# One pool of six places for the weight blocks and the transposed x, x fetched tile by tile, and the last sums in five PSUM tiles

## The chip, the cores and the metric

The kernel runs on one NeuronCore of a Trainium2 chip, in float32 throughout. The metric is the device time of one execution in microseconds (us). Three runs of the kernel before took 891.31, 893.44 and 893.68 us, so their median is 893.44. TensorE (PE in the profile, with PEld for its weight loads) does the matrix products, VectorE (DVE) most sums and transposes of 32x32 blocks, ScalarE (ACT) copies and squares, GpSimd (POOL) a share of the sums. SyncE (SP) issues the transfers (DMAs): they go out in the order of the program on SP, each waiting for its place in SBUF and for one of eight lanes, so that a DMA does not go before the DMA eight places ahead of it has landed.

## The reference: what is computed

```python
kv  = np.einsum('bhsd,bhse->bhde', k, v)          # 8 batches, 8 heads, 576 tokens, 64
out = np.einsum('bhsd,bhde->bhse', q, kv)
rms = np.sqrt(np.mean(out * out, axis=-1, keepdims=True) + 1e-06)
x   = (out / rms * g_norm)                        # put together to 4608 x 512
h   = x @ w_in                                    # 512 x 2048
g   = np.maximum(h, 0.0) ** 2
y   = g @ w_out                                   # 2048 x 512
```

Linear attention without a softmax, a norm over each head, and a two-layer network with a squared ReLU.

## The kernel before, in words

The 4608 tokens are 36 tiles of 128, and four tiles make a strip, so there are nine strips, zero to eight. Each strip goes "up" (x times w_in, then the squared ReLU) and "down" (times w_out). To save products, matrices are cut into quarters and seven products of sums take the place of eight, at one level or at two. Strip zero goes up plainly and down with one level. Strip one goes up with one level (order of the seven products: 1, 2, 6, 5, 7, 3, 4) and down with two levels, 49 small products (`down_deep`, L1084; the outer seven in `DEEP_ORDER` = 4, 1, 2, 6, 5, 7, 3, each with seven inner ones in two steps: j = 1, 2, 3 and j = 4, 5, 6, 7). Strips two to eight use two levels in both directions; their up runs in 55 slots. The attention of the strips to come, the transposes of q, the key-value products, norms and transfers are put between by lists: `slices` (L690 to L737) holds the attention's steps in order and `attend` runs the next ones; a slot plan with assumed costs decides how many go in one slot.

The first 131 us also convert the weights: sums of quarters of w_in and w_out are made on VectorE and GpSimd and stored to DRAM (w_in_deep, w_out, w_deep), from where blocks are streamed later.

`stream` (L922) asks for the next block of that stream. A block takes a place of 8 KB in each partition from `stream_pool`, which has four. A deep down needs two blocks for each outer product p: one of w_out (768 KB, for j = 3, 1, 2; called (s, p, 0) here) and one of w_deep (1 MB, for j = 5, 6, 7, 4; called (s, p, 1)). An up product of the later strips needs one block of w_in_deep (768 KB). `down_deep` calls `stream()` at each of its steps, behind that step's products (L1110).

The transposed x of a strip (`xT`, L622) has a pool of its own, two places of 8 KB in each partition, so one strip is read while the next is written. For strips zero and one TensorE transposes x (`features`, L627). From strip two on VectorE transposes blocks of 32x32 (`squares_x`), the tile goes to DRAM (`send_x`, L646, 256 KB), and later `fetch_x` (L651) brings it back with four DMAs of 64 KB in the layout that the products need. When a fetch is due is set by a clock that counts steps: 18 units after the store for the tiles of strip two, 6 for later ones. q for coming batches arrives in pairs of DMAs ("drips") when the clock allows and no fetch of x is due.

From strip one on, PSUM holds five tiles for products (`fpsum`) and two, one of double size, for the attention (`apsum`). The seven inner products of one p lie in two PSUM tiles (`PLACE`, and `LAST_PLACE` for the end of strip eight, L1040); `together` (L1061) puts them together on ScalarE and VectorE to `o_sb`, and `send` (L946) stores it. At the end of strip eight the inner products of the last p run in the groups (1), (2, 6, 5, 7), (4, 3), sums between them, and one store of 256 KB ends the kernel.

Of the kernel before, what the change touches and what calls it, by code (L numbers as in the profile page):

```python
# [10 lines left out]
FP32 = mybir.dt.float32  # L11
# [4 lines left out]
ALU = mybir.AluOpType  # L16
# [4 lines left out]
def kernel(  # L21
# [35 lines left out]
    P = 128  # L57
# [28 lines left out]
    xt_pool = ctx.enter_context(tc.tile_pool(name="xt", bufs=2))  # L86
# [4 lines left out]
    conv = ExitStack()  # L91
    raw_pool = conv.enter_context(tc.tile_pool(name="raw", bufs=8))
# [529 lines left out]
    def open_xt(s):  # L622
        if s not in xt:
            xt[s] = xt_pool.tile([P, STRIP // SQ, NP, SQ], FP32, name="xT", tag="xT")
        return xt[s]
# [20 lines left out]
    def send_x(n):  # L646
        d = sent[n] = dram.tile([P, 4, NP, SQ], FP32, name="x_d", tag="x_d", bufs=2 * NT)
        nc.sync.dma_start(out=d, in_=squared.pop(n))
        tiles_due.append((clock[0] + (6 if n >= DEEP_UP * NT + NT else 18), fetch_x, (n,)))
# [53 lines left out]
    slices += [(T, (2, 2)), (features, (last[0],)), (T, (2, 3)), (K, (2, 2, 3))]  # L703
# [239 lines left out]
    def out_tile():  # L943
        return c_pool.tile([P, 2, DH], FP32, name="o_sb", tag="c")

    def send(s, th, eh, o):  # L946
        for i, (part, t, rows) in enumerate(out_rows(NT * s + 2 * th)):
            eng = nc.scalar if i % 2 and s == N_STRIP - 1 and (th, eh) == (0, 1) else nc.sync
            eng.dma_start(out=rows[:, :, ts(eh, DH)], in_=o[part, t, :])
# [90 lines left out]
    LAST_PLACE = {1: (1, 0), 2: (0, 0), 6: (0, 1), 5: (0, 2), 7: (0, 3), 3: (1, 1), 4: (1, 2)}  # L1040
    place = lambda s, p: LAST_PLACE if s == N_STRIP - 1 and p in (5, 3) else PLACE

    def small_products(s, p, js):
        c = "B" if p in (4, 2, 5, 3) else "A"
        if js[0] == 1 and p not in (6, 7, 3):
            opened[c] = set()
            chain[c] = [fpsum.tile([P, 4, P], FP32, name=f"ps_{c}", tag="f") for _ in range(2)]
        for j in js:
            x, i = place(s, p)[j]
            a, w = leaf[p][j], w_blk.pop((s, p, j))  # L1050
            for f in range(FQ // 2):
                nc.tensor.matmul(  # L1052
                    chain[c][x][:, i, :], lhsT=a[:, f, :], rhs=w[:, f, :],
                    start=x not in opened[c] and f == 0, stop=f == FQ // 2 - 1, skip_group_check=True,
                )
            opened[c].add(x)

    def together(s, p):

        def small(j, n=1):  # L1060
            x, i = place(s, p)[j]  # L1061
            return chain["B" if p in (4, 2, 5, 3) else "A"][x][:, i : i + n]
# [12 lines left out]
        yield  # L1075
        add(q[:, 0:4:3], q[:, 0:4:3], small(3, 2))
# [7 lines left out]
    def down_deep(s, k, i):  # L1084
        p = DEEP_ORDER[k]
        if s == N_STRIP - 1 and k == 6 and i == 1:

            steps = together(s, p)
            for js in ((1,), (2, 6, 5, 7), (4, 3)):
                small_products(s, p, js)  # L1090
                next(steps)
            return
# [17 lines left out]
        stream()  # L1110
# [187 lines left out]
    for s in range(N_STRIP):  # L1298
# [25 lines left out]
        for i, (w, fn, a) in enumerate(steps):  # L1324
# [16 lines left out]
            elif s == 0 and i == n_up:  # L1341
                convert(len(conversions))
                conv.close()

                stream_pool = ctx.enter_context(tc.tile_pool(name="stream", bufs=4, reuse_waits="tile"))
                sum_pool = ctx.enter_context(tc.tile_pool(name="sum", bufs=8, reuse_waits="tile"))
# [40 lines left out]
            if i == n_up:  # L1387
                stream(2)
            if i in (n_up + 8, n_up + 11):
                load(2, (i - n_up) // 11, nc.sync, "q")  # L1390
# [9 lines left out]
            if i == n_up + 6:  # L1400
                stream()
# [42 lines left out]
```

## Time and profile before

| what | us |
|---|---|
| median of three runs | 893.44 |
| the profiled execution's own time | 889.28 |
| span of its instructions | 887.3 |
| TensorE products, busy | 876.6 (99%) |
| TensorE weight loads, busy | 821.8 (93%) |
| VectorE, busy | 721.4 (81%) |
| ScalarE, busy | 352.3 (40%) |
| GpSimd, busy | 307.3 (35%) |

The span runs from the first to the last instruction of the profiled execution; 2.0 us lie around it. The DMA engines move 235.73 MB in it, a mean of 266 GB/s, and are busy for most of the time in every stretch. A wait is told as "engine, tile, line <- what released it: us in total, times, the longest". The chain is the work that ended last, followed back from the end; in a timeline each line has the start, the time, the engine and line, the operation and the count.

### The profile page before, as it was taken

Reading aid. Unit: us, or ns where it says so; the run is one execution under the profiler, and the core shown is the slowest. Engines: PE = TensorE matmul, PEld = TensorE weight load, DVE = VectorE, ACT = ScalarE, POOL = GpSimd, SP = SyncE. Lnnn points to the kernel's source line nnn. Section 1 sums busy time; section 2 is a strip of 40 time slices with the busy share of each in tenths; the row PEclk is TensorE's granted clock in tenths of the full one; section 3 lists DMA queues with packets and bytes.
Section 4 is the critical chain, followed back from the end, with each engine's and each line's share of the span. In section 5 each row is a group of like instructions: output and inputs, shape, how many; then the busy total and the mean of one; then the engine's idle time right before and its main releaser. Section 6 shows DMA issues by size and latency. Waiting matters only on the chain.

```text
span 887.3 us, 20876 instructions
## 1 busy us (share of the span) xinstructions
PE 876.6 (99%) x8296; PEld 821.8 (93%) x8296; DVE 721.4 (81%) x1233; ACT 352.3 (40%) x806; POOL 307.3 (35%) x315
## 2 busy tenths in 40 slices
PE   8999999999999999999999999999999999999998
PEld 7445888889999999999999999999999999999998
DVE  4999998879768986798678966897888778876886
ACT  4898242320048303740365034902491147102710
POOL 0000005610558223731474045604470447044700
PEclk9999999999999999999999999999999999999999
DMA  9998997989999888979887988898658864884385
GB/s 314 315 316 251 304 366 234 273 305 328 327 232 262 297 309 249 237 269 331 238 222 250 321 268 247 251 307 285 211 166 309 297 181 171 309 291 155 137 313 180
DMA packets 169953, 235.73 MB, mean 266 GB/s; under 512 B 79488, under 2 KB 134272, under 8 KB 161536
## 3 DMA queue, kind: packets, MB, share of 16 engines
q1 hardware_dynamic: 169696, 234.40, 82.3%
q8 instruction: 65, 1.06, 0.5%
q14 instruction: 32, 0.26, 0.1%
q10 hardware_dynamic: 160, 0.00, 0.0%
HBM read 197.66 MB, written 36.70 MB: 264 GB/s over the span
## 4 chain that ended last, share of the span: by engine, by line
PE 82%; DVE 10%; DMA 3%; ACT 3%; issue 2%; SPq 0%; POOL 0%; DVEq 0%; POOLq 0%; ACTq 0%
PE ps_B L1052 22%; PE ps_A L1248 19%; PE ps_A L1052 16%; PE ps_B L1248 9%; PE ps_C L1248 5%; PE ps_A L835 4%; PE kv_ps L432 2%; PE x_ps L468 2%; DVE w_c L269 2%; PE ps_B L835 1%; DMA w_deep<-w_t 1%; DVE w_t L289 1%; DVE wt L289 1%; PE ps_C L835 1%; DVE w_c L263 1%
## 5 line engine op out<-in xcount | busy, mean ns | idle before, releaser
L1052 PE MATMUL ps_B<-w_blk,g_s 128*128 128x128 f32 x1024 | 126.1, 275 | 0.0
L1052 PEld LDWEIGHTS ps_B<-w_blk,g_s 128*128 128x128 f32 x1024 | 120.0, 192 | 0.1
L1248 PE MATMUL ps_A<-x_l,w_in 128*128 128x128 f32 x784 | 103.8, 275 | 0.3 <-ACT snap L1265 0.3
L1052 PE MATMUL ps_B<-w_blk,gt 128*128 128x128 f32 x768 | 97.5, 275 | 1.5 <-DMA w_blk<-w_out 1.5
L289 POOL TENSOR_TENSOR x_l<-xT 128x256 f32<-128x256 f32 x21 | 15.4, 734 | 238.6 <-PE ps_A L1052 187.9
L1248 PEld LDWEIGHTS ps_A<-x_l,w_in 128*128 128x128 f32 x784 | 95.4, 192 | 0.6 <-ACT snap L1265 0.5
L1052 PE MATMUL ps_A<-w_blk,g_s 128*128 128x128 f32 x768 | 93.6, 275 | 0.0
L1052 PEld LDWEIGHTS ps_B<-w_blk,gt 128*128 128x128 f32 x768 | 91.5, 192 | 1.7 <-DMA w_blk<-w_out 1.7
L1052 PEld LDWEIGHTS ps_A<-w_blk,g_s 128*128 128x128 f32 x768 | 89.6, 192 | 0.0
L1260 POOL TENSOR_TENSOR snap<-snap,gt 128x512 f32<-128x512 f32 x35 | 45.9, 1310 | 119.2 <-ACT snap L1265 103.7
L1265 ACT COPY snap<-ps_A 128x512 f32<-128x512 f32 x63 | 36.9, 585 | 109.5 <-PE ps_A L1248 96.2
L1198 ACT ACTIVATE gt<-gt 128x512 f32<-128x512 f32 x112 | 70.1, 626 | 12.8 <-DVE gt L1260 12.6
L1052 PE MATMUL ps_A<-w_blk,gt 128*128 128x128 f32 x576 | 72.2, 275 | 0.0
L1199 ACT ACTIVATE gt<-gt 128x512 f32<-128x512 f32 x112 | 70.7, 631 | 3.6
L1052 PEld LDWEIGHTS ps_A<-w_blk,gt 128*128 128x128 f32 x576 | 68.2, 192 | 0.0
L1067 DVE TENSOR_TENSOR o_sb<-o_sb,ps_B 128x256 f32<-128x256 f32 (+1 forms) x128 | 49.4, 386 | 19.2 <-ACT o_sb L1068 11.8
L1068 ACT COPY o_sb<-ps_A 128x128 f32<-128x128 f32 x24 | 6.4, 265 | 145.7 <-PE ps_A L1052 145.7
L1154 POOL TENSOR_TENSOR w_i<-w_in 128x512 f32<-128x512 f32 x7 | 10.7, 1524 | 148.1 <-DMA q<-in_q_dram 140.8
L289 DVE TENSOR_TENSOR gt<-gt 128x2048 f32<-128x2048 f32 (+1 forms) x29 | 59.7, 2063 | 0.0
L1260 POOL TENSOR_TENSOR gt<-gt,snap 128x512 f32<-128x512 f32 x42 | 52.4, 1277 | 17.6 <-DVE snap L1260 17.4
L1248 PE MATMUL ps_B<-x_l,w_blk 128*128 128x128 f32 x392 | 52.1, 276 | 0.0
L1248 PE MATMUL ps_A<-x_l,w_blk 128*128 128x128 f32 x392 | 51.9, 275 | 0.0
(183 smaller groups left out, 1835.0 us busy)
## 6 DMA issues: line engine op xcount, KB each, us to landing
w_blk<-w_deep SPq DMA_DIRECT2D x56, 1024.0 KB, 6.5
w_blk<-w_out SPq DMA_DIRECT2D x56, 768.0 KB, 6.0
w_blk<-w_in_deep SPq DMA_DIRECT2D x49, 768.0 KB, 5.5
raw<-in_moe_w_in_dram SPq DMA_DIRECT2D x16, 512.0 KB, 7.0
raw<-in_moe_w_out_dram SPq DMA_DIRECT2D x16, 512.0 KB, 5.8
k<-in_k_dram SPq DMA_DIRECT2D x29, 256.0 KB, 5.2
v<-in_v_dram SPq DMA_DIRECT2D x29, 256.0 KB, 5.4
x_d<-x_q SPq DMA_DIRECT2D x27, 256.0 KB, 5.4
```

The source lines that it names most:

```text
L269: yield nc.vector.scalar_tensor_tensor(out=ci, in0=high, scalar=-(2**30), in1=ci, op0=ALU.bitwise_and, op1=ALU.bitwise_or)
L289: eng.tensor_tensor(out=out, in0=a, in1=b, op=ALU.subtract)
L432: nc.tensor.matmul(ps[ts(h, D), i], lhsT=a, rhs=w, start=i == 0 and c == 0, stop=c == C, skip_group_check=True)
L468: nc.tensor.matmul(ps[half, r, i, ts(p, D)], lhsT=q[row, half], rhs=kvd[b, p][row, row], start=True, stop=True)
L835: nc.tensor.matmul(bank[BANK[p]][:, i, :], lhsT=lhsT(k), rhs=rhs(k), start=p in (1, 5, 2) and i == 0 and k == 0, stop=k == n - 1, skip_gro ...
L1052: nc.tensor.matmul(chain[c][x][:, i, :], lhsT=a[:, f, :], rhs=w[:, f, :], start=x not in opened[c] and f == 0, stop=f == FQ // 2 - 1, skip ...
L1067: add = lambda out, a, b: nc.vector.tensor_tensor(out=out, in0=a, in1=b, op=ALU.add)
L1198: nc.scalar.activation(o, o, AF.Relu)
L1199: nc.scalar.activation(o, o, AF.Square)
L1248: nc.tensor.matmul(ps[:, i, :], lhsT=w, rhs=rhs, start=j in (1, 2, 5) and i == 0, stop=True, skip_group_check=True)
L1260: add = lambda eng, out, a, b: eng.tensor_tensor(out=out, in0=a, in1=b, op=ALU.add)
L1265: nc.scalar.copy(t, ps)
```

## The change

Five parts.

- Places. `xt_pool` becomes a pool of one place that lives only as long as the conversion; strip zero's x lies there. Every later x takes a place of the stream's pool, which has six places in place of four. A one-column memset on GpSimd takes the place for strip one's x as the pool opens.
- Blocks. In strip zero's down one call of `stream()` moves from step 6 to step 4; in `down_deep` one call is added at the first step and those of the last p are left out, so that each block of a deep down is asked for one step earlier. The number of blocks is the same.
- Fetches. The fetch of a tile of strip two is due at its own delay: 6 units for tile 8, 30, 36 and 24 for tiles 9, 10 and 11.
- Order. The transposes of q for the last pair of batch 2, (T, (2, 3)), come before the transposes of x of one tile, features.
- The end. The seven inner products of p = 5 and p = 3 of strip eight lie in five PSUM tiles, three of `fpsum` and two of `apsum`. The last p runs in the groups (1), (2, 6), (5, 7), (4), (3); its sums are added in place as soon as a group ends, and each quarter of 128 x 128 is stored by itself, three from SP and the last from ScalarE's queue.

```diff
--- before.py
+++ after.py
@@ -83,12 +83,12 @@
     rest_pool = ctx.enter_context(tc.tile_pool(name="rest", bufs=1))
     qt_pool = ctx.enter_context(tc.tile_pool(name="qt", bufs=NP + 1))
     xn_pool = ctx.enter_context(tc.tile_pool(name="xn", bufs=3))
-    xt_pool = ctx.enter_context(tc.tile_pool(name="xt", bufs=2))
     small = ctx.enter_context(tc.tile_pool(name="small", bufs=3))
     g_pool = ctx.enter_context(tc.tile_pool(name="g", bufs=4))
     dram = ctx.enter_context(tc.tile_pool(name="dram", bufs=1, space=bass.MemoryType.DRAM))
     c_pool = ctx.enter_context(tc.tile_pool(name="c", bufs=6))
     conv = ExitStack()
+    xt_pool = conv.enter_context(tc.tile_pool(name="xt", bufs=1))
     raw_pool = conv.enter_context(tc.tile_pool(name="raw", bufs=8))
     spare_pool = conv.enter_context(tc.tile_pool(name="spare", bufs=1))
     wtmp = conv.enter_context(tc.tile_pool(name="wtmp", bufs=4))
@@ -621,7 +621,11 @@
 
     def open_xt(s):
         if s not in xt:
-            xt[s] = xt_pool.tile([P, STRIP // SQ, NP, SQ], FP32, name="xT", tag="xT")
+            if s == 0:
+                xt[s] = xt_pool.tile([P, STRIP // SQ, NP, SQ], FP32, name="xT", tag="xT")
+            else:
+                t = stream_pool.tile([P, 4, FQ // 2, P], FP32, name="xT", tag="w_blk")
+                xt[s] = t.rearrange("p n f e -> p (n f e)").rearrange("p (a q t) -> p a q t", q=NP, t=SQ)
         return xt[s]
 
     def features(n):
@@ -646,7 +650,7 @@
     def send_x(n):
         d = sent[n] = dram.tile([P, 4, NP, SQ], FP32, name="x_d", tag="x_d", bufs=2 * NT)
         nc.sync.dma_start(out=d, in_=squared.pop(n))
-        tiles_due.append((clock[0] + (6 if n >= DEEP_UP * NT + NT else 18), fetch_x, (n,)))
+        tiles_due.append((clock[0] + {9: 30, 10: 36, 11: 24}.get(n, 6), fetch_x, (n,)))
 
     def fetch_x(n):
         s, i = divmod(n, NT)
@@ -700,7 +704,7 @@
     ready[1] = len(slices)
     T, K, last = transposed_query, key_value, query_pairs(1)[2]
     slices += [(query_means, (last,)), (K, (2, 0, 1)), (T, (2, 0)), (roots_normalized, (last,)), (T, (2, 1))]
-    slices += [(T, (2, 2)), (features, (last[0],)), (T, (2, 3)), (K, (2, 2, 3))]
+    slices += [(T, (2, 2)), (T, (2, 3)), (features, (last[0],)), (K, (2, 2, 3))]
     pair_ends = []
     for b in range(2, B):
         pairs = query_pairs(b)
@@ -944,9 +948,15 @@
         return c_pool.tile([P, 2, DH], FP32, name="o_sb", tag="c")
 
     def send(s, th, eh, o):
-        for i, (part, t, rows) in enumerate(out_rows(NT * s + 2 * th)):
-            eng = nc.scalar if i % 2 and s == N_STRIP - 1 and (th, eh) == (0, 1) else nc.sync
-            eng.dma_start(out=rows[:, :, ts(eh, DH)], in_=o[part, t, :])
+        for part, t, rows in out_rows(NT * s + 2 * th):
+            nc.sync.dma_start(out=rows[:, :, ts(eh, DH)], in_=o[part, t, :])
+
+    def send_quarter(s, th, eh, o, t, h, eng):
+        for part, at, rows in out_rows(NT * s + 2 * th):
+            if at.start <= t < at.stop:
+                eng.dma_start(
+                    out=rows[:, t - at.start, eh * DH + h * P : eh * DH + (h + 1) * P], in_=o[part, t, ts(h, P)]
+                )
 
     def store_deep_sums(p, w):
         if p in (6, 4):
@@ -1037,14 +1047,18 @@
 
     PLACE = {1: (0, 0), 2: (0, 1), 6: (0, 2), 5: (1, 0), 7: (1, 1), 3: (1, 2), 4: (1, 3)}
 
-    LAST_PLACE = {1: (1, 0), 2: (0, 0), 6: (0, 1), 5: (0, 2), 7: (0, 3), 3: (1, 1), 4: (1, 2)}
+    LAST_PLACE = {1: (0, 0), 2: (1, 0), 6: (1, 1), 5: (2, 0), 7: (2, 1), 4: (3, 0), 3: (4, 0)}
     place = lambda s, p: LAST_PLACE if s == N_STRIP - 1 and p in (5, 3) else PLACE
 
     def small_products(s, p, js):
         c = "B" if p in (4, 2, 5, 3) else "A"
         if js[0] == 1 and p not in (6, 7, 3):
             opened[c] = set()
-            chain[c] = [fpsum.tile([P, 4, P], FP32, name=f"ps_{c}", tag="f") for _ in range(2)]
+            n = 2 + (s == N_STRIP - 1 and p == 5)
+            chain[c] = [fpsum.tile([P, 4, P], FP32, name=f"ps_{c}", tag="f") for _ in range(n)]
+            if n == 3:
+                chain[c].append(apsum.tile([P, 2, 4, P], FP32, name="ps_x", tag="x", bufs=1)[:, 0])
+                chain[c].append(apsum.tile([P, 4, P], FP32, name="ps_at", tag="at"))
         for j in js:
             x, i = place(s, p)[j]
             a, w = leaf[p][j], w_blk.pop((s, p, j))
@@ -1073,6 +1087,10 @@
         if p == 3:
             add(o, o, part[6])
         yield
+        if s == N_STRIP - 1 and p == 5:
+            for j, i in ((4, 3), (3, 0)):
+                add(q[:, i], q[:, i], small(j)[:, 0])
+            return
         add(q[:, 0:4:3], q[:, 0:4:3], small(3, 2))
         if p == 3:
             send(s, 0, 1, o)
@@ -1083,12 +1101,28 @@
 
     def down_deep(s, k, i):
         p = DEEP_ORDER[k]
+        if k == i == 0:
+            stream()
         if s == N_STRIP - 1 and k == 6 and i == 1:
 
-            steps = together(s, p)
-            for js in ((1,), (2, 6, 5, 7), (4, 3)):
+            o = out_tile()
+            q, rest = (t.rearrange("p t (h e) -> p (t h) e", h=2) for t in (o, part[6]))
+            at = {j: chain["B"][x][:, i : i + 1] for j, (x, i) in place(s, p).items()}
+            sums = {
+                1: [(slice(0, 4), 1)], 6: [(slice(1, 2), 2), (slice(2, 4), 6), (slice(0, 1), 6)],
+                7: [(slice(2, 3), 5), (slice(2, 3), 7), (slice(0, 1), 5), (slice(3, 4), 7)],
+                4: [(slice(3, 4), 4)], 3: [(slice(0, 1), 3)],
+            }
+            for js in ((1,), (2, 6), (5, 7), (4,), (3,)):
                 small_products(s, p, js)
-                next(steps)
+                for to, j in sums[js[-1]]:
+                    n = to.stop - to.start
+                    nc.vector.tensor_tensor(
+                        out=q[:, to], in0=rest if j == 1 else q[:, to], in1=at[j].to_broadcast([P, n, P]), op=ALU.add
+                    )
+                    if (j, to.start) in ((2, 1), (7, 2), (4, 3), (3, 0)):
+                        eng = nc.scalar if j == 3 else nc.sync
+                        send_quarter(s, 0, 1, o, *divmod(to.start, 2), eng)
             return
         if k == 0 and s >= DEEP_UP:
             if i == 0:
@@ -1107,7 +1141,8 @@
             return
         if s < N_STRIP - 1 or k < 6:
             small_products(s, p, ((1, 2, 3), (4, 5, 6, 7))[i])
-        stream()
+        if k < 6:
+            stream()
         q11, q12, q21, q22 = (gq[s, q] for q in (11, 12, 21, 22))
         if i == 1:
             if k == 0:
@@ -1342,7 +1377,7 @@
                 convert(len(conversions))
                 conv.close()
 
-                stream_pool = ctx.enter_context(tc.tile_pool(name="stream", bufs=4, reuse_waits="tile"))
+                stream_pool = ctx.enter_context(tc.tile_pool(name="stream", bufs=6, reuse_waits="tile"))
                 sum_pool = ctx.enter_context(tc.tile_pool(name="sum", bufs=8, reuse_waits="tile"))
             if s == 0 and n_up <= i < n_up + 2:
                 for g in range(2 * (i - n_up), 2 * (i - n_up) + 2):
@@ -1385,7 +1420,10 @@
                     stream()
                 continue
             if i == n_up:
+                nc.gpsimd.memset(open_xt(1)[:, 0, 0, 0:1], 0.0)
                 stream(2)
+            if i == n_up + 4:
+                stream()
             if i in (n_up + 8, n_up + 11):
                 load(2, (i - n_up) // 11, nc.sync, "q")
             if i == n_up + 12:
@@ -1397,8 +1435,6 @@
             n = i + 1 - (n_up - 6)
             pairs, m = divmod(max(n - 2 * NP, 0), 3)
             attend(min(ready[0] + min(max(n, 0), 2 * NP) + (n >= 2 * NP) + 4 * pairs + (0, 2, 2)[m], goal))
-            if i == n_up + 6:
-                stream()
             while deep_due and i not in (n_up + 1, n_up + 4, n_up + 12, n_up + 13):
                 deque(store_deep_sums(*deep_due.popleft()), 0)
             if i == n_up + 2:
```

## The prediction

> **What bounds the kernel now.** I read the page first: busy times, the 40 slices, the chain by line. All three say TensorE. The next question is what TensorE still waits for: the view of that engine's waits.
>
> ```profile
> PE 876.6 (99%) x8296; PEld 821.8 (93%) x8296; DVE 721.4 (81%) x1233; ACT 352.3 (40%) x806; POOL 307.3 (35%) x315
> ...
> PE 82%; DVE 10%; DMA 3%; ACT 3%; issue 2%; SPq 0%; POOL 0%; DVEq 0%; POOLq 0%; ACTq 0%
> ```
>
> ```profile
> PE ps_B L1052 <- DMA w_blk<-w_out: 1.5, 1, 1.5
> ...
> PE ps_A L835 <- DVE o_sb L1001: 0.4, 1, 0.4
> ...
> PE xt_ps L632 <- DVE x_n L563: 0.3, 1, 0.3
> ```
>
> The change adds and removes no product, so at most these waits and the ends of the span can move: 1.5 + 0.4 + 0.3 us, plus the stretch behind the last product. Busy 99% of 887.3 us leaves no more. The granted clock is 1.000 over the run, so nothing is to be won there.
>
> Third view, the chain around 200 us, which shows where the 1.5 us come from, and the timelines of the SP queue and of TensorE there:
>
> ```profile
> 199.04 0.32 SPq L939
> ...
> 199.88 5.53 DMA xT<-x_d
> 205.41 0.04 issue
> 205.45 4.83 DMA w_blk<-w_out
> 210.28 0.04 issue
> 210.33 4.73 PE ps_B L1052 x40
> ```
>
> ```profile
> 199.88 5.53 SPq L655 DMA_DIRECT2D xT<-x_d  x8
> 205.45 0.43 SPq L933 DMA_DIRECT2D w_blk<-w_out  x1
> ```
>
> A block of w_out is asked for at 205.45 because eight copies of strip two's x stand ahead of it on SP, each held until the copy eight places before it has landed. It lands 4.83 us later, 1.5 us after TensorE could have begun its products. The stretch before has empty DMA engines (last column but one is the share of the 16 DMA engines):
>
> ```profile
> 196.00:198.00 2.00, 2.00 (x19) 1.97 (x18) 1.97 (x4) 1.23 (x2) 0.00 (x0) 1.00 0.28 110
> 198.00:200.00 2.00, 2.00 (x21) 2.00 (x20) 1.93 (x4) 0.00 (x0) 0.00 (x0) 1.00 0.05 4
> ...
> 210.00:228.00 18.00, 17.67 (x158) 17.67 (x159) 16.19 (x27) 0.53 (x2) 0.00 (x0) 1.00 1.00 358
> ```
>
> So transfers are missing at 196 to 200 for want of a free place and are too many after. Fourth view, the same for the stretches at 128 us (chain) and at the end (timeline):
>
> ```profile
> 118.13 10.37 DMA w_deep<-w_t
> ...
> 131.21 0.61 DVE o_sb L1001
> 131.82 0.04 issue
> 131.87 8.25 PE ps_A L835 x37
> ```
>
> ```profile
> 883.01 0.69 DVE L1067 TENSOR_TENSOR o_sb<-o_sb 128x512 f32<-128x512 f32 x1
> 883.80 0.42 DVE L1067 TENSOR_TENSOR o_sb<-o_sb,ps_B 128x256 f32<-128x256 f32 x1
> ```
>
> **The change part by part.** All against the profiled execution, 889.28 us (span 887.3 and 2.0 around it), which is 0.47% below the median of 893.44.
>
> *Six places, blocks a step earlier, x's copies spread (strip one).* Block (1,1,1) is asked for at 199.04, when a place comes free. With xT of strip one in the pool, its place is released by the last product of strip one's up that reads it, at about 194.4 us, so this block goes about 4.4 us earlier. The next block, the late one, goes when the place of the product group before is free, about 199.0, and only tile 8's four copies are near it; tiles 9 to 11 come 30, 36 and 24 clock units after their stores. Against 205.45 that is 6.4 us earlier. Landing times of w_blk's DMAs between 190 and 245 us are 4.8 / 6.8 / 9.6 us (least, median, most), so it lands between 203.8 and 208.6. TensorE is ready at 208.8. The wait goes whole: -1.5 us. Bounds: -1.66 (start to start, a little slower pitch included) and 0. What is late next: the blocks behind it land 0.05 to 2.5 us before their use in strip one, and TensorE is now 1.5 us ahead; but the queue also starts 3.6 us sooner (3.7 us of idle DMA at 197 to 200.7 are filled) with the same bytes to move until 246, where its share is 1.00 or more. So each is earlier by more than its user. The count of blocks per strip is unchanged. Later strips have slacks of 0.14 to 0.17 us at the tightest blocks (strips five and eight) and TensorE does not wait there; a step earlier (3.2 to 3.5 us) can only help: 0.
>
> *Strip zero's down.* VectorE waits 0.46 us at 128.59 for a store of 10.37 us (chain above), because a small sum of weights is written over a tile that this store still reads. With the pool's size its place moves to one that engines freed. All that follows on VectorE moves up 0.46: its sum at 131.13, then TensorE's wait of 0.42 at 131.87. -0.46, bounds -0.59 and 0 (if another tile in that place is as late). The added POOL memset is one column; POOL is idle there, and only that place's first DMA could wait for it: 0.
>
> *T(2,3) ahead of features(8).* TensorE waits 0.29 us at 155.62 for VectorE's x_n (0.69 us, begun 154.79). With a transpose between, the four transposes of x (0.63 us) stand behind product group ps_C, ready then: -0.3, bounds -0.45 and 0. The price: q of that step landed at 161.95 and VectorE would stand for it some 2.5 us sooner. TensorE needs its result at 163.03 in any case, and the two works that VectorE would have done first (0.64 + 0.67) come after; TensorE may lose back up to 0.3. I take -0.3.
>
> *The tail.* Before, behind the last product (ends 883.46), VectorE has one add of 0.69 begun at 883.01, because three adds before stood in line (0.42, 0.42, 0.29 from 881.78), and the last add of 0.42, ended 884.22; the store is issued at 884.30 and lands 2.15 us later, and the span ends 0.85 after. After: each product has a PSUM tile of its own, its sums are made while later ones run (0.69 for the first, 0.29 to 0.42 each for the others: rows 128x128 286 ns, 128x256 420, 128x512 694), so behind the last product one add of 0.29 is left, begun 883.5 to 883.8: end 0.15 to 0.45 earlier. The last store is 64 KB in place of 256 KB; 64 KB copies of x hold the 16 engines 0.28 us and 256 KB stores 0.7 to 0.8, so another 0.2 or so: -0.5. Bounds: -1.0 (all the adds hidden) and +0.7: the only DMAs on ScalarE's queue before took 3.3 us to land against SP's 2.15, which is 1.15 more, less 0.45.
>
> The Trainium skill ("DMA: Bandwidth & Descriptors", section Bandwidth) speaks against this step and the tile by tile fetch: batch DMAs to 1 MiB or more, as 64 KB reaches 32% of the peak. By its table (0.95 us for 64 KB) the four quarters would hold the engines 3.8 us and the tail would gain nothing. The trace's 0.28 us per piece decides here, and three of the four quarters go before the last sum. The same page (Issuing engines are not separate DMA queues) holds that a DMA from ScalarE's queue runs on the same 16 engines and only saves issue time; no run so far shows a last store from there.
>
> *What the fetches move: q at the start of strip two.* The drips of q stand behind the fetches in SP's order. The second pair of q for batch 3 is issued before at 229.77 and lands 238.46 and 238.83. After, it comes behind two output stores, where before another pair is:
>
> ```profile
> 242.57 1.29 DVE L384 STREAM_TRANSPOSE qT<-q 128x512 f32<-128x512 f32 x2
> 243.79 0.67 DVE L388 STREAM_TRANSPOSE qT_rest<-q_rest 128x512 f32<-128x512 f32 x1
> ```
>
> ```profile
> 238.73 0.90 SPq L949 DMA_DIRECT2D out_dram<-o_sb  x2
> 239.68 1.24 SPq L123 DMA_DIRECT2D q<-in_q_dram  x2
> ```
>
> That pair landed at 247.19 and 247.39. TensorE needs the transposes for its x_ps products at 247.91, which is 245.66 once 1.5 + 0.46 + 0.3 are gained. Two transposes take 1.3 to 1.4 us, so a landing at X costs X + 1.4 - 245.66. With the queue 2.9 to 3.6 us ahead and two q (0.43 us each on the engines) fewer in front, X is about 243.3, give or take 0.7: VectorE waits 1.5 to 2 us there, TensorE not. Cost 0; bounds 0 and +4.1 (X = 248.4, the worst landing time near, 8.65 us, from 239.68). Behind it wait VectorE's adds of o_sb (1.26 + 0.69 + 0.42), whose bank has room of three slots.
>
> **Sum.** -1.5 - 0.46 - 0.3 - 0.5 = -2.76: 889.28 becomes 886.5, and against the median 893.44 becomes 890.7.
>
> **The rivals.**
>
> *More than that.* The runs without profile lie 2 to 4.4 us above the profiled one. If part of that is stalls at blocks that in the profile just came in time (slacks 0.05 to 0.17 us in strips one, five, eight), a block asked a step earlier takes some of it away. Half of the gap of 4.16 is 2.1: 888.6. Against: the gap may be launch and not stall; no row tells.
>
> *The wait moves to the next block.* The engines are full from 200.7 to 246, so if the earlier start is used up by copies that now fall between the blocks, the 1.5 us reappear at (1,2,1), which had 0.36 us of slack. Then -0.46 - 0.3 - 0.5 - 0.2 (a rest of the 1.5) = -1.5: 892.0.
>
> *The change doesn't do what it says.* If strip one's x is released later than its last product (its place is shared by a rotation of six), the blocks go no earlier than now, and strip zero and the tail alone remain: -1.26, 892.2. For it: place order is fixed by the rotation. Against: the block's request stands behind nothing else than that product.
>
> *Slower: q late.* The one mechanism is the q pair above. It undoes the whole gain from X = 247.0 on (2.76 = X + 1.4 - 245.66 gives 247.0). At X = 248.4 the sum is -2.76 + 4.1 = +1.4: 894.8. For it: without the queue's advance X is 247.39, +0.4. Against: the advance is 3.6 us where the engines were idle.
>
> **How the numbers follow.** About 0.3% (2.7 us) is what a measurement here tells from no change. Chances: forecast 0.45, more 0.22, moved or not done 0.17 together, q late 0.16. The forecast's 2.76 stands at that bound, and its terms reach 3.7 together, so a little over half of it counts as faster: 0.26, with the 0.22 of "more" 0.48. Slower by 0.3% comes from q late with the three small gains missing and the tail at its bad bound (-1.5 + 248.4 + 1.4 - 246.4 + 0.7 = +2.6) or X past 249.7: 0.10 of the 0.16, and 0.03 of the 0.17 if the moved wait is longer than the old. The rest, 0.39, is the same. Range: the low end is the gain bounds together (-1.66 - 0.59 - 0.45 - 1.0 = -3.7) with the 2.1 of the first rival: 893.44 - 5.8 = 887.6; the high end is q late at its bound, 894.8.
>
> **What would show it.** Right: no wait of TensorE for w_blk<-w_out near 209; DMA share well above 0.3 at 196 to 200; no wait of VectorE for w_deep<-w_t near 128; VectorE waiting for q near 241 to 243 with TensorE not; one add behind the last product and a store from ScalarE's queue at about 883.9. Wrong: a TensorE wait on w_blk a few us later in strip one; a wait of TensorE for qT or qT_rest before x_ps at 246 to 250; new waits on w_blk in strips three to eight, if six places that also hold x leave fewer blocks on their way than four and two did; a last landing over 3 us.

## The result and the profile after

The changed kernel takes 887.77 us (median of 20 runs, 886.13 to 893.69); the kernel before, beside it, 892.39 us (20 runs, 889.98 to 896.74). The ratio is 0.9953, with a 95% interval of 0.9938 to 0.9967: 4.6 us less, 2.9 to 5.5 by the interval. The forecast was 890.7, within 887.6 to 894.8.

The profiled execution took 886.17 us, with a span of 884.4, against 889.28 and 887.3 before: 3.1 us less, where the sum was 2.76. The two numbers differ: the median fell by 4.6, the trace by 3.1. Both profiled executions lie near the low end of their kernel's times above, so the 3.1 us compare a short run with a short run. Most of the experiments below are about that difference.

Engines, chain and waits of TensorE after:

```profile
PE 876.4 (99%) x8296; PEld 822.1 (93%) x8296; DVE 721.9 (82%) x1239; ACT 351.8 (40%) x805; POOL 307.6 (35%) x316
...
PE 95%; DVE 2%; ACT 2%; issue 0%; POOL 0%; DVEq 0%; POOLq 0%
```

```profile
PE ps_A L617 <- DVE rms L496: 0.5, 1, 0.5
PE ps_B L1283 <- DVE snap L1295: 0.4, 1, 0.4
PE ps_A L1283 <- ACT snap L1300: 0.3, 1, 0.3
```

The busy times are what they were, since no product was added or taken away. What moved is the chain: TensorE has 95% of it in place of 82%, and DMA's 3% and most of VectorE's 10% are gone. The three waits that the prediction showed are no longer in the list; the three lines above were there before too, at 0.4, 0.4 and 0.3 us (`rms` belongs to the norm, `snap` is the tile that holds a copied product).

SP's timeline and the chain around 200 us, and the DMA share (last column but one) in the stretch that was empty before:

```profile
194.17 0.32 SPq L943 DMA_DIRECT2D w_blk<-w_deep  x1
194.58 0.38 SPq L652 DMA_DIRECT2D x_d<-x_q  x1
198.57 0.32 SPq L937 DMA_DIRECT2D w_blk<-w_out  x1
```

```profile
202.11 6.25 PE ps_A L1066 x56
208.37 6.25 PE ps_B L1066 x56
```

```profile
196.00:198.00 2.00, 2.00 (x20) 2.00 (x20) 1.97 (x4) 1.13 (x2) 0.00 (x0) 1.00 1.04 426
198.00:200.00 2.00, 2.00 (x20) 2.00 (x20) 1.93 (x4) 0.00 (x0) 0.00 (x0) 1.00 0.99 384
```

Block (1,1,1) goes at 194.17 in place of 199.04, the late block (1,2,0) at 198.57 in place of 205.45. It lands at 203.86, 4.35 us before its use, and the groups of 56 products follow each other at 6.25 us. Ahead of the prediction it is said that the DMA engines were busy for most of the time in every stretch before the change; in these two their share was 0.28 and 0.05.

VectorE near 129 us in strip zero, before with its wait for a store of weights, and after without:

```profile
128.59 0.69 DVE L289 TENSOR_TENSOR w_t<-w_blk 128x512 f32<-128x512 f32 x1 [0.46 <-DMA w_deep<-w_t]
```

```profile
128.35 0.68 DVE L289 TENSOR_TENSOR w_t<-w_blk 128x512 f32<-128x512 f32 x1
```

The start of strip two's up on VectorE, and the end of the kernel:

```profile
240.35 0.70 DVE L384 STREAM_TRANSPOSE qT<-q 128x512 f32<-128x512 f32 x1
243.11 0.71 DVE L384 STREAM_TRANSPOSE qT<-q 128x512 f32<-128x512 f32 x1 [2.06 <-DMA q<-in_q_dram]
```

```profile
880.45 0.29 DVE L1120 TENSOR_TENSOR o_sb<-o_sb,ps_x 128x128 f32<-128x128 f32 x1
881.12 0.29 DVE L1120 TENSOR_TENSOR o_sb<-o_sb,ps_at 128x128 f32<-128x128 f32 x1 [0.39 <-PE ps_at L1066]
881.45 0.35 ACTq L957 DMA_DIRECT2D out_dram<-o_sb  x1
```

VectorE stands 2.06 us for q, which landed at 243.09, and TensorE does not notice. Behind the last product (it ends at 881.09) one add of 0.29 us is left.

### The profile page after: what moved, and what is told of

It reads as the page before. It is cut to its first block, busy times and chain, and to the rows that moved or that the text cites. A ratio compares the mean times of both kernels' runs of the same rounds, so it can differ in the third digit from the quotient of the medians.

```text
span 884.4 us, 20899 instructions
## 1 busy us (share of the span) xinstructions
PE 876.4 (99%) x8296; PEld 822.1 (93%) x8296; DVE 721.9 (82%) x1239; ACT 351.8 (40%) x805; POOL 307.6 (35%) x316
## 4 chain that ended last, share of the span: by engine, by line
PE 95%; DVE 2%; ACT 2%; issue 0%; POOL 0%; DVEq 0%; POOLq 0%
PE ps_B L1066 22%; PE ps_A L1283 19%; PE ps_A L1066 17%; PE ps_B L1283 9%; PE ps_A L839 6%; PE ps_C L1283 5%; PE ps_B L839 3%; PE kv_ps L432 2%; PE ps_A L880 2%; PE x_ps L468 2%; PE ps_C L839 2%; PE ps_C L880 2%; PE ps_B L880 1%; PE ps_A L617 1%; ACT gt L1234 0%
## 5 line engine op out<-in xcount | busy, mean ns | idle before, releaser
L1066 PE MATMUL ps_B<-w_blk,g_s 128*128 128x128 f32 x1008 | 123.9, 275 | 0.0
L1066 PEld LDWEIGHTS ps_B<-w_blk,g_s 128*128 128x128 f32 x1008 | 118.1, 192 | 0.1
L1066 PE MATMUL ps_B<-w_blk,gt 128*128 128x128 f32 x752 | 95.2, 275 | 0.0
L1066 PEld LDWEIGHTS ps_B<-w_blk,gt 128*128 128x128 f32 x752 | 89.6, 192 | 0.1
L1081 DVE TENSOR_TENSOR o_sb<-o_sb,ps_B 128x256 f32<-128x256 f32 (+1 forms) x123 | 47.5, 386 | 16.9 <-ACT o_sb L1082 12.0
L1081 DVE TENSOR_TENSOR o_sb<-o_sb,ps_A 128x256 f32<-128x256 f32 (+1 forms) x96 | 37.2, 387 | 15.1 <-ACT o_sb L1082 10.5
```

Of the source, the lines that this page charges most:

```text
L1066: nc.tensor.matmul(chain[c][x][:, i, :], lhsT=a[:, f, :], rhs=w[:, f, :], start=x not in opened[c] and f == 0, stop=f == FQ // 2 - 1, skip ...
L1081: add = lambda out, a, b: nc.vector.tensor_tensor(out=out, in0=a, in1=b, op=ALU.add)
```

## Experiments

The theory was the prediction's: six shared places and earlier requests take the wait for blocks out of strip one, and the rest is small. Against it stood: the spread of x's copies alone does it (A against B below), the earlier request does it (D), and the runs gain more than the trace because the trace of before was untypically good (C, V). All ratios are to runs of the kernel before on the same chip; they differ a little from the quotient of the two medians. A letter names a theory of the recorded expectations, and "asked for" is the time at which SP issues a block's DMA.

### Only the spread of x's copies

```diff
-        tiles_due.append((clock[0] + (6 if n >= DEEP_UP * NT + NT else 18), fetch_x, (n,)))
+        tiles_due.append((clock[0] + {9: 30, 10: 36, 11: 24}.get(n, 6), fetch_x, (n,)))
```

> The kernel before with the new delays of x's fetches alone (four places, requests and tail as before). Theory A, the eight copies ahead on SP made block (1,2,0) late: now it is asked for as soon as a place is free, when the block before the last is used up, about 202.5 instead of 205.45; it lands 4.8 to 6.8 us later, at 207.3 to 209.3, and TensorE, ready at 208.8, waits 0 to 0.5 us instead of 1.5. Profile shorter by 1.0 to 1.5 us, q pair later and VectorE waiting for it at about 243 to 247; TensorE waits there up to 2 us since nothing is asked for earlier. Theory B, the places made it late: asked for at 204 or later, wait of 1.0 or more, profile within 0.5 us of before. Theory C, runs without a kept trace have more such stalls: the median falls by over 2.5 us though the trace falls by 1.5 at most.

Measured: 891.17 us against 892.97, ratio 0.9988 (0.9975 to 1.0), so a gain is not shown. The trace (891.1) has block (1,2,0) asked for at 202.11, as A said, and no wait for it. But two later blocks of strip one are late in it:

```profile
233.19 1.16 PE L1052 MATMUL ps_A<-w_blk,gt 128*128 128x128 f32 x8 [0.52 <-DMA w_blk<-w_deep]
240.41 0.82 PE L1052 MATMUL ps_B<-w_blk,gt 128*128 128x128 f32 x5 [0.71 <-DMA w_blk<-w_deep]
```

The eight copies did make (1,2,0) late, so A is right on the request. Taking them away with four places leaves 0.52 + 0.71 = 1.23 us of waits in strip one in this trace; the second of them is at block (1,3,1), which is late in two of three traces of the kernel before as well (below). The trace has also a wait of 2.1 us for o_sb near 131, where the trace of before has 0.4: the first sign that such waits vary from run to run. With these waits it is 1.8 us longer than the trace of before, where A had it 1.0 to 1.5 us shorter. C's fall of the median by over 2.5 us did not come either.

### All but the spread

The changed kernel with the old delays (the line above, put back).

> The changed kernel with the fetch delays of before (18 for all tiles of strip two). Theory A: eight copies stand again ahead of block (1,2,0), which is asked for at 199.5 to 205 instead of 198.57 and TensorE waits 0.5 to 1.5 us near 208. Theory B: the store ahead of the copies goes at 194.6 when the DMA engines are idle, so its lane is free at about 199.5, the block is asked for by 200 and lands by 206: no wait, the time within 0.3 us of the changed kernel's 886.2 in the trace; VectorE's wait of 2.06 us for q near 241 goes too. Theory C: median of the changed kernel, 887.8, plus 0.5 or more.

Measured: 887.17 us, ratio 0.9935 (0.9923 to 0.9948), no worse than the changed kernel.

```profile
194.86 0.38 SPq L652 DMA_DIRECT2D x_d<-x_q  x1
195.29 6.76 SPq L659 DMA_DIRECT2D xT<-x_d  x8
202.15 0.38 SPq L937 DMA_DIRECT2D w_blk<-w_out  x1
```

The eight copies stand ahead of the block again and hold it to 202.15, 3.6 us later than in the changed kernel. It lands 0.84 us before its use: no wait. VectorE's wait of 2.06 us for q is gone, as B said, so the spread caused it: of the fourteen traces the eight with the new delays have that wait, at 1.5 to 4.0 us, and the six with the old delays have none. With six places the spread buys nothing that can be measured; A's wait and C's longer median did not come. B had the request by 200, so the copies hold it longer than B thought.

### All but the earlier requests

```diff
-        if k == i == 0:
-            stream()
...
-        if k < 6:
-            stream()
+        stream()
...
-            if i == n_up + 4:
-                stream()
...
+            if i == n_up + 6:
+                stream()
```

> The changed kernel with every block of the deep downs, and strip zero's extra one, asked for as late as before (one step later), six places kept. Theory A and B alike: the copies are spread and a place is free, so block (1,2,0) is asked for at about 202 to 203, lands 207 to 209: wait 0 to 0.4 us. Trace 886.2 to 887.0. If it is the earlier request that matters (theory D), TensorE waits 0.5 to 1.5 us near 208 and again for blocks at the starts of later downs, where slacks were 0.1 to 0.7 us: trace 887.5 or more, median up by 1.5 or more over 887.8.

Measured: 887.43 us, ratio 0.9944 (0.9931 to 0.9957); trace 886.68. No wait for a block; (1,2,0) was asked for at 198.84, sooner than any theory had it, and landed 4.36 us before its use. D falls: the earlier requests, too, can be left out.

### Only the six places

```diff
-    xt_pool = ctx.enter_context(tc.tile_pool(name="xt", bufs=2))
...
+    xt_pool = conv.enter_context(tc.tile_pool(name="xt", bufs=1))
...
+                t = stream_pool.tile([P, 4, FQ // 2, P], FP32, name="xT", tag="w_blk")
...
-                stream_pool = ctx.enter_context(tc.tile_pool(name="stream", bufs=4, reuse_waits="tile"))
+                stream_pool = ctx.enter_context(tc.tile_pool(name="stream", bufs=6, reuse_waits="tile"))
...
+                nc.gpsimd.memset(open_xt(1)[:, 0, 0, 0:1], 0.0)
```

> The kernel before with the six shared places alone: requests, fetch delays, order of the slices and tail as before. Theory P, the places carry the gain of the middle: VectorE has no wait for w_deep<-w_t near 129, TensorE none for o_sb near 131; block (1,1,1) goes at about 194.5, the eight copies after it, block (1,2,0) by 202.6, TensorE has no wait for w_blk in strip one, or one of at most 0.5 us. Trace 887.0 to 888.0 (886.2 plus the tail's 0.75 and the 0.3 of the slice order), median 888.5 to 889. Theory Q, early requests or the spread of the copies is needed beside the places: waits for w_blk of 0.5 to 1.5 us stay in strip one or at the start of strip two's down near 290, median 889.5 or more.

Measured: 889.18 us against 892.59, ratio 0.9960 (0.9947 to 0.9972): 3.4 us of the gain. Its trace (887.79, span 885.5):

```profile
195.15 8.58 SPq L659 DMA_DIRECT2D xT<-x_d  x8
203.83 0.38 SPq L937 DMA_DIRECT2D w_blk<-w_out  x1
```

```profile
208.67 1.60 PE L1056 MATMUL ps_B<-w_blk,gt 128*128 128x128 f32 x12 [0.16 <-DMA w_blk<-w_out]
```

Theory P holds for the waits; the request came 1.2 us later than P had it (202.6), and the median lies between P's 888.5 to 889 and Q's 889.5. The places alone carry most of the gain, and with copies and requests both as before the block is just late (0.16 us). Spread or earlier request then gives the margin: in the traces of the two runs above either was enough.

### All but places and requests

The complement: delays, slice order and tail of the change, four places and requests as before.

> The kernel before with the fetch delays, the slice order and the tail, but with four places and two for x, and the requests as before: all that the run with six places alone left out except the earlier requests. Theory P, the places carry the middle: the waits in strip zero (VectorE for w_deep<-w_t, 0.5 to 1.3 us) and strip one's later blocks (0.5 to 1.3 us near 232 to 240) stay, the wait near 209 and the one at 155 go, the tail is 0.75 us shorter; median 1.0 to 2.5 us below before, above the changed kernel by 2 or more. Rival: these small parts together make up the gain, median within 1 us of the changed kernel's 887.8.

Measured: 890.45 us against 892.72, ratio 0.9974 (0.9960 to 0.9988), 2.6 us above the changed kernel. In the trace the wait near 209 is gone and those for o_sb (0.8) and for blocks of strip two's down (0.60 and 0.96, at 289 and 294) stay. The later blocks of strip one cost 0.2 us at most here, so that part of the expectation failed. The median is where P had it, and the rival of small parts falls. And q is late in earnest:

```profile
246.52 0.71 DVE L384 STREAM_TRANSPOSE qT<-q 128x512 f32<-128x512 f32 x1 [4.01 <-DMA q<-in_q_dram]
247.16 0.67 DVE L388 STREAM_TRANSPOSE qT_rest<-q_rest 128x512 f32<-128x512 f32 x1
```

```profile
247.88 0.34 PE L468 MATMUL x_ps<-kv_all,qT_rest 64*64 64x64 f32 x8 [0.67 <-DVE qT_rest L388]
```

This is the slower rival of the prediction, at 0.67 us: the copies are spread without the queue's earlier start, which is the rival's condition. It does not always cost TensorE time. The trace of the spread alone has the same four places and delays and VectorE waits 3.25 us for q there, but TensorE, which was later by other waits, has none.

### Only the tail

```diff
-    LAST_PLACE = {1: (1, 0), 2: (0, 0), 6: (0, 1), 5: (0, 2), 7: (0, 3), 3: (1, 1), 4: (1, 2)}
+    LAST_PLACE = {1: (0, 0), 2: (1, 0), 6: (1, 1), 5: (2, 0), 7: (2, 1), 4: (3, 0), 3: (4, 0)}
...
-            for js in ((1,), (2, 6, 5, 7), (4, 3)):
+            for js in ((1,), (2, 6), (5, 7), (4,), (3,)):
```

> The kernel before with the new tail alone. My step: from the end of the last product to the end of the span 3.3 us as in the changed kernel against 3.8 before, so -0.5 us in trace and in the median (ratio 0.9994, inside its interval). Rival: the tail carries the part of the gain that the trace does not show, median lower by 1.5 or more.

Measured: 891.22 us against 892.97, ratio 0.9978 (0.9965 to 0.9991). The median fell by 1.75, more than expected, but the interval reaches to 0.8 us, and the trace says where 0.8 comes from. Behind the last product, in us:

| trace | VectorE's last add ends | last store landed | span ends |
|---|---|---|---|
| before (three traces) | 0.77 | 2.99 to 3.00 | 3.83 |
| tail alone | 0.33 | 1.94 | 3.01 |
| changed | 0.33 | 1.94 | 3.31 |

So the tail gives 0.44 us by the adds and 0.61 by the smaller store (it lands 1.58 us after issue, the 256 KB one 2.15), of which 0.2 to 0.5 are lost again after the last landing. The rest of the 1.75 is not shown to be the tail's, so the rival, which had a fall of 1.5 or more, is not excluded by the median; what speaks against it is the trace.

### The last store from SP

```diff
-                        eng = nc.scalar if j == 3 else nc.sync
+                        eng = nc.sync
```

> The changed kernel with the last quarter's store on SP too. In its trace the stores of 64 KB from SP land 1.54 us after issue and the one from ScalarE 1.58, so the landing is the same within 0.1 us; SP is free at 881.1, the sum ends 881.41, so the issue is not held. What can differ is the closing after the last landing, 1.36 us in the changed kernel against 0.84 before: if ScalarE's queue makes it longer, 0.2 to 0.5 us less, 885.7 to 886.0 in the trace; if not, the same. In the median no difference over 0.5 us.

Measured: 888.13 us, ratio 0.9952 (0.9937 to 0.9966), like the changed kernel; from the last product to the last landing 1.91 us (1.94), to the end of the span 3.27 (3.31). ScalarE's queue neither helps nor costs, and the longer closing (the time from the last landing to the end of the span) is not its doing.

### The kernel before, traced again

> The kernel before once more, for a second trace, since the first (889.28) was faster than nearly all of its runs (890 to 896). Theory V, the waits that the change removes are longer in most runs than in the trace that I read: VectorE's wait for w_deep<-w_t near 129 is 0.7 to 1.3 us instead of 0.46 and TensorE's for o_sb 1.0 to 2.1 instead of 0.4, and there are further waits for w_blk of 0.7 to 1.4 us near 239 or 291. Rival: these are as in the first trace and the added time lies in the opening before 90 us or behind the last product.

> As before_again, a third trace of the kernel before. Theory V as there; if both traces show the two waits (o_sb near 131, w_blk near 209) at over 1.0 us, the term for strip zero was sized from an untypical row.

Measured: 890.86 and 892.81 us. Waits of TensorE in the second:

```profile
PE ps_B L1052 <- DMA w_blk<-w_deep: 2.0, 2, 1.3
PE ps_B L1052 <- DMA w_blk<-w_out: 1.6, 1, 1.6
...
PE ps_A L835 <- DVE o_sb L1001: 0.8, 1, 0.8
```

```profile
240.56 1.16 PE L1052 MATMUL ps_B<-w_blk,gt 128*128 128x128 f32 x8 [1.27 <-DMA w_blk<-w_deep]
```

V holds for the blocks and fails for strip zero in these two traces. TensorE's time lost from start to start of its products, in us by place, for the three traces of before (the first is the one that I predicted from) and two of the changed kernel:

| place | 889.28 | 890.86 | 892.81 | after 886.17 | after 889.09 |
|---|---|---|---|---|---|
| near 131, o_sb in strip zero | 0.59 | 0.41 | 1.00 | 0 | 0.65 |
| 155 to 163, features and q | 0.45 | 0.45 | 0.45 | 0.25 | 0 |
| near 209, block (1,2,0) | 1.66 | 2.29 | 1.72 | 0 | 0 |
| near 239, block (1,3,1) | 0 | 0.80 | 1.44 | 0 | 0 |
| 286 to 296, strip two's down | 0.57 | 0.77 | 1.28 | 0.56 | 2.81 |
| near 562, snap | 0.47 | 0.47 | 0.48 | 0.47 | 0.50 |
| sum | 3.74 | 5.19 | 6.37 | 1.28 | 3.96 |

The trace that I read was faster than every one of the other runs of the kernel before (889.59 to 896.74). In strip one it had 1.66 us of waits; the others have 3.09 and 3.16, since block (1,3,1), which landed 0.39 us before its use in the first, is late in them. In strip zero other traces with four places and the old requests lost more near 131: 2.26 us with the spread alone, 1.96 with the tail alone, 0.97 without places and requests. The three traces of before average 890.98 us, still 1.4 below the median of 892.39, so the waits of the longer runs are not all accounted for here.

### The changed kernel, traced again

> The changed kernel once more, beside the others on the same chip. 886 to 889, median 887.8. In a second trace: no wait for w_blk in strip one (slack there 3 us or more), VectorE waiting for q near 242 without TensorE; what may vary is the wait for (2,4,0) near 287, 0 to 1.2 us, and the opening.

Measured: 887.81 us, ratio 0.9949 (0.9932 to 0.9966), the trace 889.09 (last column above). Strip one has no wait for blocks, with 4.35 us to spare at (1,2,0). But the margin of 3 us that was expected is not there at every block: (1,3,0) landed at 231.75, 0.14 us before its use, where the first trace of the changed kernel has 1.58. Strip two's down begins with two waits, longer than expected:

```profile
288.41 1.13 PE L1066 MATMUL ps_B<-w_blk,gt 128*128 128x128 f32 x8 [1.58 <-DMA w_blk<-w_out]
293.12 1.13 PE L1066 MATMUL ps_B<-w_blk,gt 128*128 128x128 f32 x8 [0.91 <-DMA w_blk<-w_deep]
```

And VectorE waits for a store of w_deep in strip zero after all, not near 129 but near 116:

```profile
DVE w_t L289 <- DMA w_deep<-w_t: 0.7, 1, 0.7
```

### Strip two's q held back

```diff
-                    quiet = n_up * 2 // 3 < i < n_up + 3 or s == DEEP and i > n_up + 9
+                    quiet = (20 if s == DEEP_UP else n_up * 2 // 3) < i < n_up + 3 or s == DEEP and i > n_up + 9
```

> The changed kernel with the q loads of strip two's up held back from slot 21 on, so that two pairs of q (256 KB in all) no longer stand ahead of block (2,4,0) and one no longer ahead of (2,4,1). In the changed kernel's traces (2,4,0) is asked for at 279.9 and lands 0.76 us before its use, or 0.0 in a slower trace (wait 1.16 us). Theory L, late blocks at the start of strip two's down are what is left: asked for 1.5 to 2 us earlier, slack 2.0 us or more, no wait for w_blk near 287 to 293; median lower by 0.3 to 0.8 us, 887.0 to 887.5. Rival: q now comes late for VectorE's transposes in strip three and TensorE waits there: median 888 or more.

Measured: 887.41 us, ratio 0.9945 (0.9927 to 0.9963): no difference from the changed kernel that can be told. In the trace, which is the slowest of its runs (891.49), (2,4,0) lands 3.24 us early, so the two waits above are gone. A wait of 1.0 us for `snap` stands near 292, and two for blocks come later:

```profile
333.39 0.82 PE L1066 MATMUL ps_B<-w_blk,gt 128*128 128x128 f32 x5 [1.19 <-DMA w_blk<-w_deep]
```

```profile
387.67 1.13 PE L1066 MATMUL ps_B<-w_blk,gt 128*128 128x128 f32 x8 [1.07 <-DMA w_blk<-w_deep]
```

L is right on the two waits. What that is worth is not shown: the median is the one that L forecast, but it lies within the spread of the changed kernel's runs. Whether the new waits come from the q loads that now go later is open.

### Strip zero's request put back

```diff
-            if i == n_up + 4:
-                stream()
...
+            if i == n_up + 6:
+                stream()
```

> The changed kernel with strip zero's one call of stream() put back from step 4 to step 6; all else as changed. The order of the requests decides which place the third sum of weights, w_t, is written over: with the call at step 4 it is the place of the second w_t, whose store lands at 115.6 to 117.5 while VectorE is there at 115.8 to 116.3 (waits of 0.7 to 1.3 us in four traces of five so requested); with the call at step 6 it is the place of the first, whose store lands at 113.1 to 115.0. Theory W, the wait for w_deep<-w_t was moved by the earlier request and not removed: here VectorE has no wait for that store near 116 nor near 129, TensorE none near 131, the span's median falls by 0.4 to 0.8 us from 886.0 to about 885.4, and the time's by as much, to 887.2. Rival: the wait at 116 comes from late stores in general: it stays, at 0.5 us or more, or shows near 129, and the median stays at 887.8.

Measured: 886.80 us (6 runs, 885.68 to 889.69) against 892.55, ratio 0.9943 (0.9926 to 0.9960). The median of the span is 884.9, where the changed kernel has 885.95 and 886.0. The trace took 886.11 us, with no wait for w_deep on VectorE and none of TensorE near 131. The five traces of kernels with the call at step 4 and six places (changed, changed again, last store from SP, q held, old delays) have waits of 0, 0.7, 1.3, 1.2 and 0.8 us near 116; the three with the call at step 6 (places alone, old requests, this one) have none. Here are VectorE's timelines of the kernel with the last store from SP, of the changed kernel, of the run with the old requests and of the spread alone:

```profile
115.54 0.68 DVE L563 TENSOR_TENSOR x_n<-x_ps,newton 128x512 f32<-128x512 f32 x1
117.50 0.69 DVE L289 TENSOR_TENSOR w_t<-w_in 128x512 f32<-128x512 f32 x1 [1.28 <-DMA w_deep<-w_t]
```

```profile
114.57 1.29 DVE L563 TENSOR_TENSOR x_n<-x_ps,newton 128x512 f32<-128x512 f32 x2
115.78 0.68 DVE L289 TENSOR_TENSOR w_t<-w_in 128x512 f32<-128x512 f32 x1
```

```profile
115.70 0.68 DVE L289 TENSOR_TENSOR w_t<-w_in 128x512 f32<-128x512 f32 x1
```

```profile
116.86 0.69 DVE L289 TENSOR_TENSOR w_t<-w_in 128x512 f32<-128x512 f32 x1 [0.85 <-DMA w_deep<-w_t]
```

W holds for the place: with six places and the call at step 4 the third w_t waits for the semaphore of the second one's store, which lands at 115.6 to 117.5; with the call at step 6 it waits for that of the first one's, which landed by 113.4. The run with the old requests shows this by its times, since VectorE begins at 115.70, before the second store lands at 115.82. The trace of this run doesn't by itself: its second store landed at 115.50, before VectorE came at 115.87.

W is wrong that the earlier request moved the wait from 129 to 116. In the kernel before, with four places and the call at step 6, the third w_t waits for the second store too. In the traces of the spread alone (last line above) and of the tail alone VectorE stood 0.85 and 0.97 us there and again near 129; in the other four with four places the second store landed 0.3 to 0.5 us before VectorE came. So the places take away both waits, and the call at step 4 lets the one at 116 stand. Why the second store lands later in some executions is open. This version has the lowest median of all that were measured; its interval overlaps the changed kernel's, so faster than it is not shown.

## Why the prediction was right, and where not

- Range and sign were right. The forecast itself, 890.7, was 2.9 us above the median measured, which lies only 0.2 us above the low end of the range. Of the 2.9 us, 1.05 come from the base, since the three runs had a median of 893.44 and twenty have 892.39; the gain was 1.9 short (2.76 for 4.62). Against its own profiled execution the sum was 0.35 us short (886.5 for 886.17). Some of that closeness is luck, as the trace of after is the one of five in which strip zero's wait did not show.
- Strip one's block, -1.5: the mechanism is right, with request (198.57 for "about 199.0") and landing (203.86, within 203.8 to 208.6) as worked out. The term is mis-sized: it was read from one trace, the fastest of all. In three traces strip one's waits are 1.66, 3.09 and 3.16, a mean of 2.6, and all of it goes. This is what the prediction had as its first rival, "more than that" (888.6, chance 0.22), with the reason given there, blocks that in the trace just came in time; it named strips one, five and eight, and it was strip one; no trace of before waited for blocks in the other two. Its doubt that the gap might be launch falls: time less span is 1.97 us at the median in the runs of before, 1.98 in the trace.
- Which part does it: the prediction gave strip one's gain to places, requests and spread together. The places alone have 3.4 of some 4.7 us, strip zero's part included; requests and spread replace each other.
- Strip zero's down, -0.46: this step failed in part. The wait near 129 went in all eight traces with six places. But in four of the five with the call at step 4 VectorE waits near 116, for the store of an earlier tile of the same kind, and TensorE's loss near 131 is 0.65 to 1.36 us in three of them. The prediction did not see this second wait, which the kernel before has too in some executions, nor that the moved request in strip zero lets it stand. With six places and the call at step 6 TensorE lost nothing there in three traces.
- T(2,3) ahead of features, -0.3: 0.45 went; in the trace of after 0.25 came back at 163 (the prediction had up to 0.3), in the second trace nothing.
- Tail, -0.5: 0.52 in the span. The part of the adds was 0.44 (0.15 to 0.45), the store gave 0.61 by landing (0.2), and 0.5 of it was lost after the last landing, which the prediction did not have, so that the sum fits is in part luck. The bound of +0.7 from ScalarE's queue was far off: 1.58 us to landing, SP's own 64 KB stores 1.53 to 1.54.
- q at the start of strip two, 0: right, X was 243.09 for 243.3, VectorE's wait 2.06 for 1.5 to 2, TensorE's none. The rival is real, as the run without places shows, but at 0.67 us and not at 4.1.
- Later strips, 0: that a step earlier "can only help" is not shown for the start of strip two's down. TensorE lost 0.56 and 2.81 us there in the changed kernel's two traces, 0.57 to 1.28 in the three of before.
- The Trainium skill ("DMA: Bandwidth & Descriptors", Bandwidth) spoke for fewer, larger transfers. In the tail the 64 KB store is the better one, 1.58 against 2.15 us to landing, and only the last one's landing stands on the path. The page's other statement (Issuing engines are not separate DMA queues) agrees with the last store taking the same time from either queue.

## What to carry to other kernels

A wait sized from one trace is a sample: a block that lands within half a microsecond of its use may be late in the next run, as (1,3,1) was here, so list the near misses, count them with the wait that is seen, and trace the kernel more than once. Sharing one pool between tiles with different lives brought more here than reordering requests, but the order of the requests then also decides whose place a tile takes: look for tiles that are written over a place whose store is still on its way. Of parts that each give the same margin one is enough, and another can do harm, as the earlier request in strip zero let a wait stand that the places alone take away.

## What the runs showed of the hardware

The time of a run less its span is the same in nearly all runs of a kernel, but differs between kernels: 1.97 us before, 1.8 in the changed kernel, 2.27 with the old requests or with places alone (medians of the runs). From the last landing to the end of the span it took 0.84 us before, 1.37 in the changed kernel and 1.07 with the tail alone, though these last two end with the same stores. No run here tells why, and both are of the size of the terms above, so spans and times should not be mixed in one sum. A store of 1 MB of weights issued at about 118 to 122 us landed 9.3 to 12.1 us later in the fourteen traces, and one issued at 107 to 108 us 7.5 to 9.4 us later.
